# Linear attention feeding a two-layer MLP on one core: batch 1's kv put between its transposes, its denominators and scaling earlier, two loads exchanged

## The chip, the core and the metric

One core of a Trainium2 chip. Its engines run side by side, each with its own queue of instructions that it works off in order: TensorE (PE, matmuls; PEld are its weight loads), VectorE (DVE), ScalarE (ACT), GpSimd (POOL) and SyncE (SP). They meet through semaphores. Matmul results land in PSUM, which this kernel uses as 8 banks of 128 partitions by 512 float32. Transfers between DRAM and the on-chip memory go through 16 DMA engines; a transfer is put in a queue by one of the engines above, and a transfer that converts float32 to bfloat16, as all loads here do, is put in by GpSimd.

The metric is device time of the core in microseconds (us), as the median of several runs.

## The reference: what is computed

Eight batches, 8 heads, 576 positions, head size 64. First linear attention, then, with the heads laid side by side to 4608 tokens of 512 features, two matrix products with a tanh between.

```python
def phi(x):
    return np.where(x > 0, x, np.exp(x) - 1.0) + 1.0
q_p, k_p = (phi(q), phi(k))
kv = np.einsum('bhsd,bhse->bhde', k_p, v)
z = np.sum(k_p, axis=2)
num = np.einsum('bhsd,bhde->bhse', q_p, kv)
den = np.einsum('bhsd,bhd->bhs', q_p, z)[..., None] + 1e-06
x = (num / den)                      # to [4608, 512]
h = x @ w_in                         # [512, 2048]
out = (h - np.tanh(h)) @ w_out       # [2048, 512]
```

## The kernel before

**Two grids that don't match.** Attention works by batch, 576 tokens each (B = 8). The MLP works by chunk `c` of 512 tokens (NC = 9). `xT` holds the attention's result, features on partitions, in four slices `p` of 128 features: two heads each, the "pairs" of this text. Chunk 0 needs batch 0, chunk 1 needs the last 64 tokens of batch 0 and most of batch 1, and so on. So while chunk `c` runs, the attention of batch `c + 1` is made between its matmuls, and phi of batch `c + 2` is begun.

**A chunk.** Layer 1 (`l1mm`, line 366) has 16 blocks `fi`; a block is four matmuls, one for each pair `p`, into one PSUM bank. From chunk 1 on two blocks fill two neighbouring banks, ScalarE makes the tanh of both at once (line 372) and VectorE subtracts (line 373), which writes `gT` and sets the two banks free. Six banks (0 to 5) go round this way; banks 6 and 7 are attention's. Layer 2 (`l2mm`, line 387) has 16 steps `s` of four matmuls each, in lists `s2[s]` that name what is to be issued after the step. In chunk 0 the step is `(g, i)` = (`s // 4`, `s % 4`): the first four steps use the first quarter of `w_out`, steps 4 to 7 the second, steps 8 to 11 the third, steps 12 to 15 the last, and from step 12 on each step ends with a copy of a finished bank to `osb` on ScalarE (line 396) and two stores from SyncE's queue. In later chunks a bank is finished before the next is begun.

**Batch 1**, whose order is written out by hand into chunk 0's lists: phi of k and q; `a_qT_pe(1, i)` (line 157), 9 transposes on TensorE for each half `i` of q, copied out by ScalarE (line 168) and VectorE (line 170); `a_kv(1)` (line 180), 36 matmuls over k and v, masked into `kz` by VectorE (line 186); `b0_scale_rest` (line 261), the last 64 tokens of batch 0; `a_den` (line 267), 16 matmuls, an addition and a reciprocal; `num1` (line 516), 8 matmuls copied to `ns` by ScalarE; `a_split` (line 288), four VectorE instructions that split the reciprocal into parts in bfloat16; `spread1(h)` (line 511), 8 matmuls that spread the reciprocals of two pairs over the partitions (line 354), and two VectorE products (line 359) that write these pairs of `xT`. These use banks 4 to 7 in turn (`side`).

**Batch 2**, also by hand: `phi_pieces` (line 121) gives three parts for half a tensor: an exp on ScalarE (line 134), a maximum on VectorE (line 135) and a minimum on VectorE (line 136). `exp2` issues the first, `rest2` the other two. `a_qT_dma(2)` (line 151) puts a transposing DMA into SyncE's queue. A tiny GpSimd copy (`gate`, line 380) waits for it, and behind it GpSimd issues the loads of batch 3. `a_kv_cols(2)` (line 191) and `a_den(2)` follow within layer 1 of chunk 1; `a_spread` (line 301) sends the reciprocals of batch 2 through DRAM and back, and line 328 multiplies them into `xT` during layer 2 of chunk 1.

**The loads.** GpSimd's queue holds, among others and in this order: q, k, v of batch 0, `w_in`, k of batch 1, quarters 0 and 1 of `w_out`, q of batch 1, quarter 2 of `w_out`, v of batch 1, quarter 3 of `w_out`; then q, k, v of batch 2, once phi of batch 1's q is done with its buffer.

**The beginning of chunk 1.** Blocks 0 and 1 are interleaved (line 581): pairs 0 and 1 of both, then pairs 2 and 3 of both, so that the later pairs are asked for later.

Of the kernel before, what the change touches and what calls it, by code (L numbers as in the profile page):

```python
# [18 lines left out]
def kernel(  # L19
# [14 lines left out]
    NP = H // 2  # L34
# [17 lines left out]
    ps_all = psum.tile([128, 8, 512], F32, name="ps_all")  # L52
# [9 lines left out]
    dense = Banks([0, 1, 2, 3, 4, 5])  # L62
# [41 lines left out]
    def load_v(b):  # L104
        load(b, v_b[b % 2][:, 0:2], v, b == 0)
# [8 lines left out]
    def load_wo(g):  # L114
        nc.gpsimd.dma_start(out=w_out_sb[:, 4 * g:4 * g + 4, :],
                            in_=moe_w_out[512 * g:512 * g + 512, :].rearrange("(ko ki) f -> ki ko f", ki=128))
# [40 lines left out]
    def a_qT_pe(b, i, banks, on=None):  # L157
        if i == 0:
            new_qT(b)
        for n in range(2):  # L160
            j0, j1 = ((0, 5), (5, 9))[n]
            ps = banks().bitcast(BF16).rearrange("p (j t) -> p j t", t=128)
            for j in range(j0, j1):
                nc.tensor.transpose(ps[:, j - j0, :], qp_t[b][:, i, j].rearrange("p h d -> p (h d)"), ident)
            src = ps[:, 0:j1 - j0, :]
            dst = qT_t[b][:, i, j0:j1].rearrange("p j g t -> p j (g t)")
            if (on or "AV")[n] == "A":
                nc.scalar.copy(dst, src)
            else:
                nc.vector.tensor_copy(dst, src)  # L170
# [9 lines left out]
    def a_kv(b, banks):  # L180
        kz_t[b] = kz_c[b % 2]
        ps = [banks()[:, 0:384].rearrange("p (i e) -> p i e", i=2) for hg in range(2)]
        for i in range(2):
            kv_mm(b, i, [ps[hg][:, i, :] for hg in range(2)])
        for hg in range(2):
            nc.vector.tensor_mul(kz_t[b][:, hg], ps[hg][:, :, 0:160], mask[:, hg])
# [74 lines left out]
    def b0_scale_rest(banks):  # L261
        ps = num_mm(0, NP, banks)
        nc.vector.tensor_mul(
            xT[:, :, 512:576].rearrange("p a (t c) -> p a t c", t=4),
            ps[:, 0:NP, :].rearrange("p a (t c) -> p a t c", t=4), rdb_t[0])
# [22 lines left out]
    def a_split(b):  # L288

        f = rden_t[b]  # L290
        t1 = rpool.tile([128, J * 16], BF16, name="t1")
        u = rpool.tile([128, J * 16], F32, name="u")
        t2 = rpool.tile([128, J * 16], BF16, name="t2")
        w = rpool.tile([128, J * 16], BF16, name="w")
        nc.vector.tensor_copy(t1, f)
        nc.vector.scalar_tensor_tensor(u, t1, part[:, 0:1], f, ALU.mult, ALU.add)
        nc.vector.tensor_copy(t2, u)
        nc.vector.scalar_tensor_tensor(w, t2, part[:, 1:2], u, ALU.mult, ALU.add)
        rden_t[b] = w
# [118 lines left out]
    for i in (1, 0):  # L418
        nc.gpsimd.memset(v_b[i][:, 2], 1.0)
    nc.gpsimd.memset(vp[:, :, :, 128:136], 1.0)  # L420
    load_wo(2)
    load_v(1)
    load_wo(3)

    nc.vector.memset(mask, 0.0)
# [76 lines left out]
    for c in range(NC):  # L502
        gT = gpool.tile([128, NF, 512], BF16, name="gT")
        n1, n2 = c + 1, c + 2
        s1 = {i: [] for i in range(16)}
        s2 = {i: [] for i in range(16)}
        if c == 0:
            side = Banks([4, 5, 6, 7])
            sub = {}

            def spread1(h):
                sub["bp"] = a_spread_pe(1, 4, (2 * h, 2 * h + 1))
                for p in (2 * h, 2 * h + 1):
                    a_scale(1, p, sub["ns"], sub["bp"], 144 * (p % 2))

            def num1():
                sub["ns"] = new_ns(1)
                for p in (NP, 0, 1, 2, 3):
                    a_num_copy(1, sub["ns"], p, side)

            s1[11].append(lambda: a_kphi(1, 0))
            s1[13].append(lambda: a_kphi(1, 1))
            s2[3].append(lambda: a_qphi(1, 0))
            s2[4].append(lambda: (a_qphi(1, 1), load_q(2), load_k(2), load_v(2)))
            s2[0].append(prepare)
            s2[7].append(lambda: a_qT_pe(1, 0, side))
            s2[8].append(lambda: a_qT_pe(1, 1, side))
            s2[10].append(lambda: (a_kv(1, side), b0_scale_rest(side)))
            s2[11].append(lambda: (a_den(1, side), num1(), a_split(1)))
            s2[13].append(lambda: spread1(0))  # L530

            qs, ks = [], []

            def exp2(pieces, src, store, name, i):
                pieces.append(phi_pieces(2, src, store, name, i))
                pieces[i][0]()

            def rest2(f):
                f[1]()
                f[2]()  # L540

            s2[12].append(lambda: exp2(qs, q_t, qp_t, "qp", 0))
            s2[13].append(lambda: exp2(qs, q_t, qp_t, "qp", 1))
            s2[14].append(lambda: exp2(ks, k_t, kp_t, "kp", 0))
            s2[15].append(lambda: (spread1(1), rest2(qs[0]), rest2(qs[1]), a_qT_dma(2), rest2(ks[0])))
        elif n1 < B:
            s1[8 if c == 1 else 5].append(lambda: a_kv_cols(n1, attn))
            s1[10 if c == 1 else 8].append(lambda: (a_den(n1, attn), a_spread(n1)))
            for p in range(NP + 1):
                s2[(11 if c == 1 else 9) + p].append(lambda p=p: a_num(n1, p))  # L550
        if c == 1:
            s1[1].append(lambda: a_kphi(2, 1))
            s1[3].append(lambda: (a_vp(2, 0), a_vp(2, 1)))
        if c >= 1 and n2 < B:

            s1[0].append(lambda: (gate(qT_t[n1]), load_k(n2), load_q(n2), load_v(n2)))
            d = 2
            s2[d].append(lambda: a_kphi(n2, 0))
            s2[d + 2].append(lambda: a_kphi(n2, 1))
            s2[d + 4].append(lambda: a_qphi(n2, 0))  # L560
            s2[d + 6].append(lambda: (a_qphi(n2, 1), a_qT_dma(n2)))
            for i in range(2):
                s2[14 + i].append(lambda i=i: a_vp(n2, i))
        if c == 0:

            first = Banks([4, 5, 6, 7, 0, 1, 2, 3])
            hs = [ps_all[:, n, :] for n in range(4)]
            order = [((0, 0), (0, 1)), ((2, 0), (2, 1), (0, 2), (0, 3), (2, 2), (2, 3)),
                     [(p, fi) for p in (1, 3) for fi in range(4)]]
            seen = [0] * 4  # L570
            for n, part_ in enumerate(order):
                if n == 1:
                    open2()
                for p, fi in part_:
                    l1mm(c, fi, hs[fi], p, seen[fi])
                    seen[fi] += 1
            for fi in range(4):
                l1act(fi, hs[fi], gT)
        for fi in range(4 if c == 0 else 0, NF):
            h = first() if c == 0 else dense()  # L580
            if c == 1 and fi == 1:
                for two in (0, 2):
                    for f, o in ((0, ps_all[:, dense.order[(dense.n - 2) % 6], :]), (1, h)):
                        for p in (two, two + 1):
                            l1mm(c, f, o, p, p)
            elif c != 1 or fi > 1:
                for p in range(NP):
                    l1mm(c, fi, h, p, p)
            if c == 0:
                l1act(fi, h, gT)  # L590
            elif fi % 2:
                n = dense.order[(dense.n - 1) % 6]
                l1act2(fi - 1, ps_all[:, n - 1:n + 1, :], gT)
            for f in s1[fi]:
                f()
        os_ = {}
        for s in range(16):

            (g, i) = divmod(s, 4) if c == 0 else (s % 4, s // 4)
            if g == 0:  # L600
                os_[i] = ps_all[:, i, :] if c == 0 else dense()
            if c == NC - 1 and i == 3:

                if g == 0:
                    o2 = dense()
                    for o, f in ((os_[i], slice(0, 384)), (o2, slice(384, DM))):
                        for fi in range(NF):
                            nc.tensor.matmul(o[:, f], gT[:, fi, 384:512], w_out_sb[:, fi, f],
                                             start=(fi == 0), stop=(fi == NF - 1))
                        evac(c, i, o, f.start, f.stop)  # L610
                continue
            l2mm(gT, os_[i], i, 4 * g, 4 * g + 4)
            if g == 3:
                evac(c, i, os_[i])
            for f in s2[s]:
                f()
# [30 lines left out]
```

## Time and profile before

| | |
|---|---|
| median of 3 runs | 295.46 us (295.45 to 295.57) |
| the profiled execution | 295.57 us |
| its span, first to last instruction | 293.8 us |
| TensorE busy | 283.4 us |
| VectorE busy | 174.6 us |
| ScalarE busy | 139.4 us |
| GpSimd busy | 33.4 us |
| bytes moved by DMA | 38.94 MB, 133 GB/s over the span |

The span in 40 slices of 7.3 us, in tenths of busy time, for TensorE, VectorE, ScalarE and the DMA engines; the last row but one is the clock granted to TensorE:

```
PE   7899999899999999999999999999999999999994
DVE  4759948997467764786478646866581446106600
ACT  3838538747334653455246524661452155126411
PEclk9999999999999999999999999999999999999999
DMA  6999999878989658945796669767107310131032
```

A line of the timeline gives the start in us, the time from the first start to the last end, the engine, the line of the kernel, the operation, what it writes and reads, and how many instructions are merged. In brackets stand the engine's idle time before it and what ended it. "DMA_DIRECT2D" lines of POOL or SP are the issue of a transfer; the transfer lands later, and the list of DMA issues gives the time from issue to landing.

Chunk 0's layer 2 runs from 31.3 us to 50.2 us, layer 1 of chunk 1 from there to 67.6 us, and its layer 2 to 82.8 us. From then on a chunk with attention in it takes 30.4 us (113.1 to 143.5 us).

### The profile page before, as it was taken

How to read it: one execution, taken by the hardware profiler on the slowest of the kernel's cores; microseconds unless marked ns; L12 is line 12 of the kernel's file. 1: busy time of each engine (PE TensorE's matmuls, PEld its weight loads, DVE VectorE, ACT ScalarE, POOL GpSimd, SP SyncE). 2: the span in 40 equal slices, each digit the busy share in tenths (PEclk: the TensorE clock that was granted, in tenths of full speed). 3: DMA queues.
4: the chain of work that ended last, by engine and by line, in shares of the span. 5: the costliest groups of instructions: out<-in, count | busy, mean ns of one | idle time of the engine just before them, and what ended most of it. 6: DMA issues, size and time to landing. Idle time of an engine off the chain costs nothing.

```text
span 293.8 us, 4475 instructions
## 1 busy us (share of the span) xinstructions
PE 283.4 (96%) x1773; PEld 133.9 (46%) x1801; DVE 174.6 (59%) x265; ACT 139.4 (47%) x168; POOL 33.4 (11%) x55
## 2 busy tenths in 40 slices
PE   7899999899999999999999999999999999999994
PEld 2544464344445444444454445444544444444443
DVE  4759948997467764786478646866581446106600
ACT  3838538747334653455246524661452155126411
POOL 8573030030030003000300021000000000000000
PEclk9999999999999999999999999999999999999999
DMA  6999999878989658945796669767107310131032
GB/s 96 195 204 213 207 207 219 203 118 161 231 167 194 145 122 140 221 112 130 137 218 118 155 137 174 143 149 149 38 21 180 73 36 0 38 82 25 0 74 71
DMA packets 39077, 38.94 MB, mean 133 GB/s; under 512 B 16336, under 2 KB 33808, under 8 KB 38288
## 3 DMA queue, kind: packets, MB, share of 16 engines
q0 software_dynamic: 17552, 18.35, 38.6%
q1 hardware_dynamic: 21344, 20.17, 30.1%
q8 instruction: 14, 0.23, 0.3%
q10 hardware_dynamic: 160, 0.13, 0.1%
q14 instruction: 7, 0.06, 0.1%
HBM read 43.91 MB, written 9.55 MB: 182 GB/s over the span
## 4 chain that ended last, share of the span: by engine, by line
PE 80%; DMA 9%; DVE 5%; ACT 2%; issue 1%; POOL 1%; SPq 1%; DVEq 0%; ACTq 0%; POOLq 0%
PE ps_all L366 37%; PE ps_all L387 35%; DMA rdb<-ds 3%; DMA v<-in_v_dram 2%; DMA out_dram<-osb 2%; PE ps_all L199 2%; PE ps_all L317 2%; DMA ds<-rden 1%; PE ps_all L276 1%; DVE gT L378 1%; DVE gT L373 1%; ACT th L377 1%; ACT osb L396 1%; PE ps_all L177 1%; DVE qp L136 1%
## 5 line engine op out<-in xcount | busy, mean ns | idle before, releaser
L366 PE MATMUL ps_all<-xT,w_in_sb 128*128 128x512 bf16 x561 | 127.5, 379 | 2.5 <-DVE gT L373 1.1
L387 PE MATMUL ps_all<-w_out_sb,gT 128*128 128x512 bf16 x547 | 126.0, 379 | 0.7
L373 DVE TENSOR_TENSOR gT<-ps_all,th 128x1024 bf16<-128x1024 f32 x64 | 77.9, 1218 | 59.3 <-ACT th L372 59.3
L372 ACT ACTIVATE th<-ps_all 128x1024 f32<-128x1024 f32 x64 | 65.5, 1024 | 58.4 <-PE ps_all L366 45.4
L366 PEld LDWEIGHTS <-w_in_sb 128*128 128x128 bf16 x576 | 55.1, 98 | 68.4 <-issue 3.0
L387 PEld LDWEIGHTS <-gT 128*128 128x128 bf16 x560 | 54.2, 98 | 64.5 <-issue 0.5
L396 ACT COPY osb<-ps_all 128x512 f32<-128x512 f32 (+1 forms) x36 | 21.2, 589 | 72.4 <-PE ps_all L387 56.0
L328 DVE TENSOR_TENSOR xT<-ps_all,rdb 128x512 bf16<-128x512 f32 x24 | 16.3, 690 | 13.8 <-PE ps_all L317 11.2
L134 ACT ACTIVATE e<-qraw 128x1152 bf16<-128x1152 bf16 x16 | 18.6, 1168 | 6.7 <-DMA qraw<-in_q_dram 6.7
L134 ACT ACTIVATE e<-kraw 128x1152 bf16<-128x1152 bf16 x15 | 17.5, 1166 | 0.4 <-DMA kraw<-in_k_dram 0.4
L136 DVE TENSOR_TENSOR qp<-e,r 128x1152 bf16<-128x1152 bf16 x16 | 12.1, 758 | 8.1 <-ACT e L134 7.3
L136 DVE TENSOR_TENSOR kp<-e,r 128x1152 bf16<-128x1152 bf16 x15 | 11.4, 758 | 7.9 <-ACT e L134 7.0
L383 POOL COPY g<-qT 1x1 bf16<-1x1 bf16 x5 | 1.2, 241 | 121.4 <-DMA qT<-qp 121.4
L378 DVE TENSOR_TENSOR gT<-ps_all,th 128x512 bf16<-128x512 f32 x16 | 10.3, 686 | 2.4 <-ACT th L377 1.7
L377 ACT ACTIVATE th<-ps_all 128x512 f32<-128x512 f32 x16 | 9.2, 599 | 4.3 <-PE ps_all L366 3.1
L317 PE MATMUL ps_all<-qT,kz 128*128 128x512 bf16 x28 | 10.1, 379 | 0.2 <-DVE xT L328 0.2
L444 PE MATMUL ps_all<-zero 128*128 128x512 bf16 x29 | 8.3, 443 | 1.2 <-DVE zero L405 1.2
L135 DVE TENSOR_SCALAR r<-qraw 128x1152 bf16<-128x1152 bf16 x16 | 7.3, 454 | 2.1 <-DMA qraw<-in_q_dram 2.1
L199 PEld LDWEIGHTS <-kp 64*128 64x128 bf16 x216 | 6.4, 94 | 2.5 <-issue 2.1
L285 DVE RECIPROCAL rden<-den 128x144 f32<-128x144 f32 x7 | 7.4, 1053 | 0.2
L199 PE MATMUL ps_all<-vp,kp 64*128 64x136 bf16 x216 | 7.4, 220 | 0.0
L394 DVE COPY osb<-ps_all 128x128 f32<-128x128 f32 x1 | 0.3, 292 | 11.6 <-DMA out_dram<-osb 11.6
(82 smaller groups left out, 121.5 us busy)
## 6 DMA issues: line engine op xcount, KB each, us to landing
out_dram<-osb SPq DMA_DIRECT2D x70, 128.0 KB
rdb<-ds SPq DMA_DIRECT2D x12, 576.0 KB
kraw<-in_k_dram POOLq DMA_DIRECT2D x7, 576.0 KB, 7.1
qraw<-in_q_dram POOLq DMA_DIRECT2D x7, 576.0 KB, 9.1
v<-in_v_dram POOLq DMA_DIRECT2D x7, 576.0 KB, 12.2
w_out_sb<-in_moe_w_out_dram POOLq DMA_DIRECT2D x4, 512.0 KB, 15.0
w_in_sb<-in_moe_w_in_dram POOLq DMA_DIRECT2D x6, 256.0 KB, 8.6
qraw<-in_q_dram POOLq DMA_DIRECT2D x2, 288.0 KB, 4.7
```

What stands on the lines that cost most here:

```text
L134: return (lambda: nc.scalar.activation(e, x, AF.Exp), lambda: nc.vector.tensor_scalar(r, x, 0.0, 1.0, ALU.max, ALU.add), lambda: nc.vector ...
L136: lambda: nc.vector.tensor_tensor(y, e, r, ALU.min))
L199: nc.tensor.matmul(ps[hg][:, i, :], kp[r, i, j].rearrange("p h d -> p (h d)"), vp[r, i, j, :], start=(j == 0), stop=(j == J - 1))
L317: nc.tensor.matmul(ps, kz[:, p // 2, p % 2, 0:128], qT[:, p % 2, 0:8, p // 2, :], start=True, stop=True)
L328: nc.vector.tensor_mul(xT[:, p, S * b:S * b + 512].rearrange("p (j t c) -> p j t c", j=8, t=4), ps.rearrange("p j (t c) -> p j t c", t=4), ...
L366: nc.tensor.matmul(h, w_in_sb[:, 2 * (p % 2) + p // 2, fi * 128:(fi + 1) * 128], xT[:, p, c * 512:(c + 1) * 512], start=(n == 0), stop=(n ...
L372: nc.scalar.activation(th, h, AF.Tanh)
L373: nc.vector.tensor_sub(gT[:, fi:fi + 2, :], h, th)
L377: nc.scalar.activation(th, h, AF.Tanh)
L378: nc.vector.tensor_sub(gT[:, fi, :], h, th)
L387: nc.tensor.matmul(o, gT[:, fi, i * 128:(i + 1) * 128], w_out_sb[:, fi, :], start=(fi == 0), stop=(fi == NF - 1))
L396: nc.scalar.copy(osb[:, f0:f1], o[:, f0:f1])
```

## The change

The two loads change places. In chunk 0's lists, kv of batch 1 goes between the two groups of transposes and all three go behind step 7 (before: transposes behind steps 7 and 8, kv behind step 10). The rest of batch 0 goes from behind step 10 to behind step 8, den, num and split from 11 to 9, the spreads from 13 and 15 to 11 and 13. Of batch 2, exp of q's first half goes from behind step 12 to behind 11, q's second from 13 to 12, k's first from 14 to 13; the VectorE parts, which all came behind step 15 after the second spread's products, now come behind the step of their exp or the one after, q's first half ahead of the second spread's products; the transposing DMA goes from behind step 15 to behind step 13, ahead of the stores of two finished banks. In chunk 1, blocks 0 and 1 of layer 1 are no longer interleaved. No instruction is added or taken away on any engine.

```diff
+    load_v(1)
     load_wo(2)
-    load_v(1)
     load_wo(3)
...
-            s2[7].append(lambda: a_qT_pe(1, 0, side))
-            s2[8].append(lambda: a_qT_pe(1, 1, side))
-            s2[10].append(lambda: (a_kv(1, side), b0_scale_rest(side)))
-            s2[11].append(lambda: (a_den(1, side), num1(), a_split(1)))
-            s2[13].append(lambda: spread1(0))
+            s2[7].append(lambda: (a_qT_pe(1, 0, side), a_kv(1, side), a_qT_pe(1, 1, side)))
+            s2[8].append(lambda: b0_scale_rest(side))
+            s2[9].append(lambda: (a_den(1, side), num1(), a_split(1)))
+            s2[11].append(lambda: spread1(0))
...
-            s2[12].append(lambda: exp2(qs, q_t, qp_t, "qp", 0))
-            s2[13].append(lambda: exp2(qs, q_t, qp_t, "qp", 1))
-            s2[14].append(lambda: exp2(ks, k_t, kp_t, "kp", 0))
-            s2[15].append(lambda: (spread1(1), rest2(qs[0]), rest2(qs[1]), a_qT_dma(2), rest2(ks[0])))
+            s2[11].append(lambda: (exp2(qs, q_t, qp_t, "qp", 0), rest2(qs[0])))
+            s2[12].append(lambda: exp2(qs, q_t, qp_t, "qp", 1))
+            s2[13].append(lambda: (spread1(1), exp2(ks, k_t, kp_t, "kp", 0), rest2(qs[1]), a_qT_dma(2)))
+            s2[14].append(lambda: rest2(ks[0]))
...
-            if c == 1 and fi == 1:
-                for two in (0, 2):
-                    for f, o in ((0, ps_all[:, dense.order[(dense.n - 2) % 6], :]), (1, h)):
-                        for p in (two, two + 1):
-                            l1mm(c, f, o, p, p)
-            elif c != 1 or fi > 1:
-                for p in range(NP):
-                    l1mm(c, fi, h, p, p)
+            for p in range(NP):
+                l1mm(c, fi, h, p, p)
```

## The prediction

> **What bounds the kernel now.** I read the busy line and the chain first, then the timelines of TensorE (PE) and VectorE (DVE) where the diff acts, 38 to 63 us, then the landings of the loads, then TensorE from 63 us to the end for what could swallow a gain.
>
> ```profile
> PE 283.4 (96%) x1773; PEld 133.9 (46%) x1801; DVE 174.6 (59%) x265; ACT 139.4 (47%) x168; POOL 33.4 (11%) x55
> PE 80%; DMA 9%; DVE 5%; ACT 2%; issue 1%; POOL 1%; SPq 1%; DVEq 0%; ACTq 0%; POOLq 0%
> ```
>
> TensorE is the bound: only its pauses can be won or lost. From 98.31 to 106.94 us 40 dense matmuls start in a row, so one takes 8.63 / 40 = 0.2158 us from start to start (the 0.38 us printed for one overlaps its neighbours). With that pitch I find the pauses; the bracketed idle time is 0.16 us short of each.
>
> ```profile
> 38.19 0.67 PE L164 MATMUL ps_all<-ident,qp 128*128 128x128 bf16 x9
> 41.88 1.66 PE L177 MATMUL ps_all<-v,kp 64*128 64x192 bf16 x36
> 44.56 0.43 PE L276 MATMUL ps_all<-qT,kz 128*32 128x144 bf16 x16
> 47.85 0.30 PE L354 MATMUL ps_all<-w,sel 32*128 32x144 bf16 x8
> 50.15 1.30 PE L366 MATMUL ps_all<-xT,w_in_sb 128*128 128x512 bf16 x5
> 51.74 4.26 PE L366 MATMUL ps_all<-xT,w_in_sb 128*128 128x512 bf16 x19 [0.29 <-DVE xT L359]
> 56.58 1.89 PE L366 MATMUL ps_all<-xT,w_in_sb 128*128 128x512 bf16 x8 [0.57 <-DVE gT L373]
> 58.94 1.02 PE L366 MATMUL ps_all<-xT,w_in_sb 128*128 128x512 bf16 x4 [0.48 <-DVE gT L373]
> 62.90 0.43 PE L276 MATMUL ps_all<-qT,kz 128*32 128x144 bf16 x16
> 80.48 0.38 PE L317 MATMUL ps_all<-qT,kz 128*128 128x512 bf16 x1 [0.20 <-DVE xT L328]
> ```
>
> Chunk 1 begins at 50.15. Five matmuls end their turn at 50.15 + 5 x 0.2158 = 51.23, the next starts at 51.74: 0.51 lost, waiting for scaled xT of pair 3. Then 51.74 + 19 x 0.2158 = 55.84 against 56.58: 0.74 lost; 56.58 + 8 x 0.2158 = 58.31 against 58.94: 0.63 lost; both wait until VectorE's L373 frees a pair of banks. Another 0.10 goes before L199 at 59.90. Sum 1.98 us. VectorE shows why:
>
> ```profile
> 48.27 1.42 DVE L359 TENSOR_TENSOR xT<-ns,ps_all 128x576 bf16<-128x576 f32 x2 [0.48 <-PE ps_all L354]
> 50.27 1.42 DVE L359 TENSOR_TENSOR xT<-ns,ps_all 128x576 bf16<-128x576 f32 x2 [0.58 <-PE ps_all L354]
> 55.31 1.22 DVE L373 TENSOR_TENSOR gT<-ps_all,th 128x1024 bf16<-128x1024 f32 x1
> 57.67 1.22 DVE L373 TENSOR_TENSOR gT<-ps_all,th 128x1024 bf16<-128x1024 f32 x1
> ```
>
> From 50.27 it has no gap until past 60 us: two scales, three phi pieces, L373, a phi piece, L373. It idles 0.58 us before 50.27, and its whole load hangs on when the spreads (L354) come. After 63 us TensorE has one pause worth naming, at 80.48: the step before starts at 79.25, four matmuls end at 80.11, so 0.37 is lost until the reciprocals have come back from DRAM (L328).
>
> **The loads.** They come down GpSimd's queue in order:
>
> ```profile
> 22.59 0.75 POOL L115 DMA_DIRECT2D w_out_sb<-in_moe_w_out_dram  x1
> 23.32 0.76 POOL L93 DMA_DIRECT2D v<-in_v_dram  x1
> ...
> w_out_sb<-in_moe_w_out_dram POOLq DMA_DIRECT2D x1, 512.0 KB, 15.8
> v<-in_v_dram POOLq DMA_DIRECT2D x1, 576.0 KB, 17.9
> ```
>
> Issue plus landing: q of batch 1 at 19.70 + 16.1 = 35.80, third quarter of w_out at 22.59 + 15.8 = 38.39, v of batch 1 at 23.32 + 17.9 = 41.22, last quarter at 24.05 + 19.7 = 43.75. So w_out takes 2.59 after its forerunner and v takes 2.83.
>
> **The change, part by part.** Swapping the two loads puts v at 35.80 + 2.83 = 38.63 and the third quarter at 41.22; the last quarter stays at 43.75, and q, k, v of batch 2 behind it keep their 46.6, 49.6 and 52.6. TensorE's work is the same set of matmuls in another order, so I walk it. First transposes at 38.19 as before, done 38.70. kv (36 matmuls, 41.88 to 43.48 = 1.60, and 0.09 lead-in): v has landed 0.07 earlier; done 40.39. Its waits for the copies out of the transposes' banks (ScalarE, VectorE done by 39.4) lie under it. Second transposes to 40.89. Step 8 needs the third quarter: 41.22 and a wake-up of 0.04, (q of batch 1: landed 35.80, used 35.83), so 41.26, **a new pause of 0.37**. Behind it in TensorE's queue stand step 8 and everything else. Step 8 to 42.12, four small matmuls for the rest of batch 0 (0.12), step 9 to 43.10, den from 43.15 (44.56 before). VectorE's masks of kz and the second copy of qT are done by 41.7, so nothing waits for them. Rest of num 0.12 and four num 0.86, steps 10 and 11: 46.2. The spread comes 47.85 - 44.56 = 3.29 after den (reciprocal and split), at 46.44; the pause of 0.2 there is as large before (45.92 + 8 x 0.2158 = 47.65 against 47.85), so it cancels. Steps 12, 13 to 48.40, second spread 0.23, steps 14, 15 to 50.36: chunk 1 starts **0.21 later** than 50.15, the 0.37 less the small waits that go.
>
> VectorE starts its scales 0.42 after the spread (48.27 - 47.85), at 46.86, and is past two at 48.16. Then the new order puts phi of q ahead of the other two: 1.23 a piece (51.61 to 52.84). Its exp needs q at 46.6 and 1.16 on ScalarE, done 47.8, so nothing is late; if q came after 47.6 the delay would pass to pair 2. Scales of pairs 2 and 3 from 49.4 to 50.8. TensorE wants them at 50.36 + 0.43 = 50.79 and 51.01, and they are there at 50.1 and 50.8: so the interleaving of the first two blocks goes at no cost, on a slack of 0.2; without it the price is again some tenths. Then phi to 53.15, L373 from 53.3 (its tanh ends 53.3, after the output copies of ScalarE), phi, L373 from 55.66 to 56.88. TensorE needs these banks at 50.36 + 24 x 0.2158 = 55.54 (free at 54.5) and 57.27 (free at 56.88). No pause. The copies of v end 57.6, ahead of L199 at 58.1. den of batch 2 starts at 61.13 instead of 62.90: **1.77 earlier** = 1.98 - 0.21. ScalarE's exps move ahead of output copies; its queue then runs 46.6 to 55.2 nearly full, with 0.3 to spare before the tanh. SyncE's transpose of q passes four store issues and starts at 52.0 instead of 54.23; the stores behind its 2.81 us feed only free output buffers. The gate at L383 and the loads of batch 3 follow some 2 us earlier, beside a chain of den that is 1.8 earlier too.
>
> What the trace does not show is the round trip of the reciprocals in its new place. Before: reciprocal done 65.73, landed in DRAM 71.06, back at 79.6. It starts 1.8 earlier and so do the loads it shares the engines with. Bounds: landing unmoved takes all 1.77 back; the pause of 0.37 gone gives 2.14. I take the same pause, since both shift together. The third quarter's landing is bounded by 38.4 and 43.75, the landings about it; I take 41.22, the sum of spacings.
>
> A rule that speaks against the change. The granted clock stood at 1.00 through transposes and small matmuls:
>
> ```profile
> 39.00:42.00 3.00, 3.00 (x25) 1.51 (x25) 0.78 (x3) 1.06 (x2) 1.92 (x3) 1.00 1.23 207
> 42.00:45.00 3.00, 2.95 (x62) 2.06 (x60) 1.22 (x3) 0.00 (x0) 0.00 (x0) 1.00 1.22 207
> ```
>
> (length, PE, PEld, DVE, ACT, POOL busy, clock, DMA share, GB/s.) The Trainium skill, "TensorE: Matmul & The Clock Gate", section "What's actually happening", has the clock halve after an idle window of about 3.4 us, and its Part 4 says that transposes do not count as busy. From 38.19 to 41.26 the new order has 3.07 us without a dense matmul, so the page leaves it just warm; should it trip, an estimate by that page is some 1.7 us lost, and the sum would be near zero. The trace has no such stretch, and I keep 1.00.
>
> **Sum.** The profiled execution took 295.57: span 293.80 and 1.77 around it. Minus 1.77 is 293.80; the median of the runs, 295.46, is 0.11 below the profiled one, so the forecast is 293.7.
>
> **Rivals.** (1) The round trip decides. At 80.48 TensorE already waits for it, which speaks for; that the chain and its competing loads both start about 2 us earlier speaks against. Half the shift lost gives 294.6, all of it 295.46: no change. (2) Slower: v keeps its landing. TensorE's queue is in order, and kv now stands ahead of steps 8 to 11, which before ran under that load. Each tenth that v comes after 39.0 (38.63 and the slack of 0.37) costs a tenth; past 40.8 the change loses. At the old 41.22 kv ends at 42.96, transposes 43.46, step 8 is 2.20 late: 293.7 + 2.2 = 295.9. Seven landings in queue order, 2.3 to 2.9 apart, speak against it; that TensorE arrives 0.07 after the estimate speaks for it.
>
> **How the numbers follow.** A measurement of this kernel tells about 0.2% (0.6 us) from no change. Forecast 0.62, its own range 293.2 (a smaller round-trip pause) to 294.4 (some tenths at the thin margins). Rival 1 gets 0.18: 0.10 still faster, 0.08 no change. Rival 2 gets 0.20, slower or a hair under. Faster 0.72, same 0.08, slower 0.20. The range runs to 295.8, over rival 1 and the near part of rival 2, and down to 293.1.
>
> **What would show it.** Right: L177 from about 38.7, one pause near 41.2 on the third quarter, no bracket on L373 before L366 between 50 and 60 us, L276 of batch 2 near 61.1, every later stage 1.8 earlier. Wrong: L177 well past 39; scales of pair 3 after 51.0; a longer wait for L328 near 78; a clock under 1.00 about 41 us.

## The result, and the profile after

| | before | after |
|---|---|---|
| median | 295.50 us (295.45 to 295.57, 4 runs) | 293.98 us (293.58 to 294.60, 4 runs) |
| the profiled execution | 295.57 us, span 293.8 us | 293.58 us, span 291.8 us |

The ratio is 0.995, with a 95% interval of 0.9929 to 0.9971: 1.5 us faster. Over all three sets of the changed kernel (15 executions, the experiments' among them) the median is 294.01.

The page's line of busy time, and its chain by engine:

```profile
PE 283.9 (97%) x1772; PEld 134.2 (46%) x1801; DVE 174.7 (60%) x265; ACT 139.6 (48%) x168; POOL 33.4 (11%) x55
PE 81%; DMA 14%; POOL 2%; issue 1%; ACT 1%; SPq 0%; DVE 0%; POOLq 0%
```

The work is the same; the span around it is 2.0 us shorter. VectorE, 5% of the chain before, has gone from it. In its place stands DMA with 14%: the chain now goes back from step 8 to the landing of the third quarter of `w_out`. The timeline of TensorE of the changed kernel, at the places shown of before:

```profile
37.78 0.67 PE L164 MATMUL ps_all<-ident,qp 128*128 128x128 bf16 x9
38.58 1.66 PE L177 MATMUL ps_all<-v,kp 64*128 64x192 bf16 x36
40.17 0.68 PE L164 MATMUL ps_all<-ident,qp 128*128 128x128 bf16 x9
41.08 1.02 PE L387 MATMUL ps_all<-w_out_sb,gT 128*128 128x512 bf16 x3 [0.24 <-DMA w_out_sb<-in_moe_w_out_dram]
...
46.30 0.30 PE L354 MATMUL ps_all<-w,sel 32*128 32x144 bf16 x8
...
50.34 7.93 PE L366 MATMUL ps_all<-xT,w_in_sb 128*128 128x512 bf16 x35
58.21 1.24 PE L199 MATMUL ps_all<-vp,kp 64*128 64x136 bf16 x36
...
61.21 0.43 PE L276 MATMUL ps_all<-qT,kz 128*32 128x144 bf16 x16
...
78.48 0.38 PE L317 MATMUL ps_all<-qT,kz 128*128 128x512 bf16 x1
```

What to see: the four stretches of L366 between 50 and 60 us, with a bracket between each, have become one line of 7.93 us that no bracket cuts (36 matmuls at 0.2158 take 7.77 from start to start, and one record is missing). The new pause stands at 41.08, with its DMA named: the transposes end their turn at 40.17 + 0.51 = 40.68, so 0.40 are lost. VectorE's timeline shows why the others went:

```profile
46.73 1.42 DVE L359 TENSOR_TENSOR xT<-ns,ps_all 128x576 bf16<-128x576 f32 x2 [0.48 <-PE ps_all L354]
48.06 0.45 DVE L135 TENSOR_SCALAR r<-qraw 128x1152 bf16<-128x1152 bf16 x1
...
49.30 1.41 DVE L359 TENSOR_TENSOR xT<-ns,ps_all 128x576 bf16<-128x576 f32 x2
...
53.33 1.23 DVE L373 TENSOR_TENSOR gT<-ps_all,th 128x1024 bf16<-128x1024 f32 x1
...
55.70 1.22 DVE L373 TENSOR_TENSOR gT<-ps_all,th 128x1024 bf16<-128x1024 f32 x1
```

The scales start 1.54 earlier than at 48.27, the gap of 0.58 between their pairs is filled with a phi piece, and L373 starts 1.98 earlier, while chunk 1 starts 0.19 later. The loads, from the list of DMA issues (v issued at 22.46, the quarter at 23.19):

```profile
v<-in_v_dram POOLq DMA_DIRECT2D x1, 576.0 KB, 16.1
w_out_sb<-in_moe_w_out_dram POOLq DMA_DIRECT2D x1, 512.0 KB, 17.9
```

They land at 38.56 and 41.09 by these rounded figures, and TensorE's kv and step 8 start at 38.58 and 41.08: between 38 and 41 us TensorE follows the load queue. One thing shows how firmly. In this execution k and v of batch 0 landed some 0.4 earlier than in the profile of before, so chunk 0's layer 2 began at 30.88 instead of 31.29 and the first transposes came at 37.78 instead of 38.19. Nothing of it was left at 41.08: kv, due at 37.78 + 0.51 + 0.09 = 38.38, waited 0.20 for v, and step 8 the 0.40.

### The profile page after: what moved, and what is told of

Its sections match the earlier page's. It is cut to its first block, busy times and chain, and to the rows that moved or that the text cites. A ratio compares the mean times of both kernels' runs of the same rounds, so it can differ in the third digit from the quotient of the medians.

```text
span 291.8 us, 4470 instructions
## 1 busy us (share of the span) xinstructions
PE 283.9 (97%) x1772; PEld 134.2 (46%) x1801; DVE 174.7 (60%) x265; ACT 139.6 (48%) x168; POOL 33.4 (11%) x55
## 4 chain that ended last, share of the span: by engine, by line
PE 81%; DMA 14%; POOL 2%; issue 1%; ACT 1%; SPq 0%; DVE 0%; POOLq 0%
PE ps_all L366 38%; PE ps_all L387 37%; DMA w_out_sb<-in_moe_w_out_dram 6%; DMA w_in_sb<-in_moe_w_in_dram 3%; DMA out_dram<-osb 2%; PE ps_all L199 2%; DMA kraw<-in_k_dram 2%; PE ps_all L317 2%; PE ps_all L276 1%; POOL v L419 1%; ACT osb L396 1%; SPq L401 0%; POOL qraw L90 0%; PE ps_all L320 0%; POOL qraw L93 0%
## 5 line engine op out<-in xcount | busy, mean ns | idle before, releaser
L366 PE MATMUL ps_all<-xT,w_in_sb 128*128 128x512 bf16 x560 | 127.1, 380 | 1.1 <-DVE xT L244 0.3
L373 DVE TENSOR_TENSOR gT<-ps_all,th 128x1024 bf16<-128x1024 f32 x64 | 77.9, 1218 | 59.8 <-ACT th L372 59.6
L366 PEld LDWEIGHTS <-w_in_sb 128*128 128x128 bf16 x576 | 55.1, 98 | 66.8 <-issue 0.6
L328 DVE TENSOR_TENSOR xT<-ps_all,rdb 128x512 bf16<-128x512 f32 x24 | 16.3, 690 | 13.5 <-PE ps_all L317 13.5
L444 PE MATMUL ps_all<-zero 128*128 128x512 bf16 x29 | 9.2, 482 | 1.2 <-DVE zero L405 1.2
L317 PE MATMUL ps_all<-qT,kz 128*128 128x512 bf16 x28 | 10.1, 380 | 0.0
L199 PEld LDWEIGHTS <-kp 64*128 64x128 bf16 x216 | 6.4, 94 | 2.5 <-issue 2.5
L199 PE MATMUL ps_all<-vp,kp 64*128 64x136 bf16 x216 | 7.4, 220 | 0.0
```

The lines of the kernel that those rows point to most:

```text
L199: nc.tensor.matmul(ps[hg][:, i, :], kp[r, i, j].rearrange("p h d -> p (h d)"), vp[r, i, j, :], start=(j == 0), stop=(j == J - 1))
L317: nc.tensor.matmul(ps, kz[:, p // 2, p % 2, 0:128], qT[:, p % 2, 0:8, p // 2, :], start=True, stop=True)
L328: nc.vector.tensor_mul(xT[:, p, S * b:S * b + 512].rearrange("p (j t c) -> p j t c", j=8, t=4), ps.rearrange("p j (t c) -> p j t c", t=4), ...
L366: nc.tensor.matmul(h, w_in_sb[:, 2 * (p % 2) + p // 2, fi * 128:(fi + 1) * 128], xT[:, p, c * 512:(c + 1) * 512], start=(n == 0), stop=(n ...
L373: nc.vector.tensor_sub(gT[:, fi:fi + 2, :], h, th)
```

## The experiments

Every kernel was timed beside the kernel before on the same chip; a ratio is to that one. "The changed kernel" is the version of the diff.

### 1. The changed kernel again, twice

No edit.

> The changed kernel once more, to see how far its times spread (293.58 to 294.60 in four runs, where the kernel before kept within 0.12). Theory: TensorE now meets v of batch 1 and the third quarter of w_out as they land, so the spread of the landings passes to the end: 293.6 to 294.6 again, and if the profiled execution falls high, step 8 starts later than 41.08 us by as much. Rival: the first four runs were a matter of that chip or hour: all within 0.2 of each other.

> The changed kernel, as the measure for the two variants run beside it: 293.9, with a pause of some 0.35 to 0.4 before step 8 and of 0.1 to 0.3 before kv.

Measured: 293.85 (293.44 to 294.35), ratio 0.9945 [0.9932, 0.9957], and 294.01 (293.56 to 294.34), ratio 0.9953 [0.9942, 0.9965]. The gain is firm. The theory of the spread isn't borne out: beside these the kernel before spread from 294.95 to 295.89 and from 295.07 to 295.75, as wide as the changed one, though nothing in it waits for v or the third quarter. Its 0.12 in the first runs were the exception. In the profiles of the two kv starts at 38.74 and 38.81 and step 8 at 41.19 and 41.14, den of batch 2 at 61.31 and 61.27. There the transposes came later (38.15 and 38.21), so kv did not wait for v, against the second expectation, and the pause before step 8 was 0.35 and 0.23.

### 2. The loads in their old order, the rest as changed (run twice)

```diff
-    load_v(1)
     load_wo(2)
+    load_v(1)
     load_wo(3)
```

> The changed kernel with the third quarter of w_out ahead of v of batch 1 again, the rest as changed. Theory (loads land in queue order, and kv now stands first in TensorE's queue): kv starts at 41.2 instead of 38.58, step 8 at 43.4 instead of 41.08, everything later: 294.0 + 2.3 = 296.3. Rival (the two loads are served side by side, the order matters little): within 0.5 of the changed kernel.

> The changed kernel with the loads in their old order once more. In six runs it took 295.8 to 296.2 twice and 297.4 to 297.7 four times, and the granted clock fell to 0.991 to 0.994 in the latter. Theory: the pause of 2.5 before kv, with transposes on one side and kv on the other, lets the clock fall to half for one stretch of some 3.5 us in which TensorE loses 1.6 to 1.8; if the profiled execution is of these, the rows show the clock at 0.5 between 41 and 49 us and matmuls of twice the time. Rival: the clock falls only behind the last matmul, and the 1.6 come from later landings: then kv starts near 42.6.

Measured: 297.37 (295.79 to 297.66), ratio 1.0059 [1.0042, 1.0077], and 297.34 (295.92 to 297.58), ratio 1.0061 [1.0044, 1.0078]. The timeline of TensorE in the first:

```profile
41.07 1.66 PE L177 MATMUL ps_all<-v,kp 64*128 64x192 bf16 x36 [2.51 <-DMA v<-in_v_dram]
...
43.17 1.03 PE L387 MATMUL ps_all<-w_out_sb,gT 128*128 128x512 bf16 x4
...
52.44 7.93 PE L366 MATMUL ps_all<-xT,w_in_sb 128*128 128x512 bf16 x36
```

kv waits for v by name, and step 8 is 2.1 late: landing follows queue order, as the theory had it (it forecast 296.3; the medians are 1 us above that). That accounts for the profiled execution, 295.79, which is 2.1 above the 293.65 of the changed kernel's profile beside it. But both profiled executions were the fastest of their six, and eight of the twelve took about 1.5 more, each with a mean granted clock of 0.991 to 0.994 where the four others have 0.997 to 1.00. The second run was to catch one of these in its profile and didn't, so where the clock fell in them is not shown; experiment 3 was made for it.

### 3. v of batch 1 behind both quarters: a longer pause

```diff
-    load_v(1)
     load_wo(2)
     load_wo(3)
+    load_v(1)
```

> The changed kernel with v of batch 1 behind both last quarters of w_out, so that kv waits longer still: v lands near 43.6, kv starts there after a pause of 5.2, step 8 near 45.8, 4.7 later than in the changed kernel. Theory (a pause of this length always lets the clock fall): the granted clock shows 0.5 in the rows from some point after 41 us, matmuls of twice the time follow for up to 4 us, and the whole is 294.0 + 4.7 + 1.7 = 300.4. Rival (the clock has no part in it): 298.7, clock 1.00 throughout.

Measured: 300.39 (300.04 to 301.37), ratio 1.0174 [1.0159, 1.0190]. The table by stretches has length, busy time of PE, PEld, DVE, ACT and POOL, the granted clock, the share of DMA and GB/s:

```profile
38.00:40.00 2.00, 0.77 (x10) 0.50 (x9) 1.50 (x4) 0.99 (x2) 1.06 (x2) 1.00 1.24 207
40.00:42.00 2.00, 0.00 (x0) 0.00 (x0) 0.00 (x0) 0.00 (x0) 1.17 (x2) 1.00 1.21 208
42.00:44.00 2.00, 0.00 (x0) 0.00 (x0) 0.00 (x0) 0.00 (x0) 0.00 (x0) 0.71 1.22 208
44.00:46.00 2.00, 1.97 (x26) 1.86 (x28) 0.00 (x0) 0.00 (x0) 0.00 (x0) 0.50 1.21 207
46.00:48.00 2.00, 2.00 (x24) 1.66 (x21) 0.88 (x2) 0.22 (x1) 0.00 (x0) 0.50 1.21 206
48.00:50.00 2.00, 1.78 (x10) 0.79 (x10) 0.45 (x3) 0.47 (x1) 0.00 (x0) 0.58 1.21 209
50.00:52.00 2.00, 2.00 (x28) 0.97 (x27) 1.15 (x3) 0.56 (x2) 0.00 (x0) 1.00 0.57 100
```

and from its timeline of TensorE:

```profile
44.03 3.06 PE L177 MATMUL ps_all<-v,kp 64*128 64x192 bf16 x36 [5.26 <-DMA v<-in_v_dram]
47.03 1.14 PE L164 MATMUL ps_all<-ident,qp 128*128 128x128 bf16 x9
```

The clock falls to half within the pause. A mean of 0.71 means that 0.58 of the stretch from 42 to 44 was at 0.5, so it fell at 42.84, and 0.58 from 48 to 50 means that it came back at 49.68: 6.8 us at half speed, in which the 36 matmuls of kv take 3.06 instead of 1.66. den of batch 1 starts at 50.74 against 43.02, 7.7 later: 5.45 are the later start of kv, less the 0.40 of the pause before step 8 that no longer occurs, and 2.7 are the clock. The forecast of 300.4 was met by the median alone: the profiled execution, 301.37, is the slowest, and in it both terms were larger (5.05 instead of 4.7 for the later start, 2.7 instead of 1.7 for the clock). All four executions have a mean clock of 0.986 or 0.987. So a pause of 5.3 brought the clock down in all four; the pause of 2.5 in experiment 2, by the mean clocks of its list, in eight executions of twelve.

### 4. The kernel before, with the loads exchanged

```diff
-    load_wo(2)
     load_v(1)
+    load_wo(2)
     load_wo(3)
```

> The kernel before with only the two loads exchanged. Theory: step 8, which stands between its two groups of transposes, waits for the third quarter until 41.1 instead of starting at 38.7, v is early for nothing, all else 2.3 later: 297.7, and up to 1.6 more in executions where the clock falls. So neither the loads nor the order of the matmuls gains alone. Rival (an earlier v is what gains): below 295.4.

Measured: 298.58 (297.60 to 299.88), ratio 1.0111 [1.0090, 1.0131]; the profiled execution 297.60, the lowest; three of six have a mean clock of 0.993, and with 298.95 to 299.88 they are the three slowest.

```profile
40.97 1.02 PE L387 MATMUL ps_all<-w_out_sb,gT 128*128 128x512 bf16 x4 [2.75 <-DMA w_out_sb<-in_moe_w_out_dram]
...
54.01 4.26 PE L366 MATMUL ps_all<-xT,w_in_sb 128*128 128x512 bf16 x19 [0.29 <-DVE xT L359]
58.84 1.89 PE L366 MATMUL ps_all<-xT,w_in_sb 128*128 128x512 bf16 x8 [0.57 <-DVE gT L373]
```

Step 8 waits, and the brackets of the kernel before come back to the hundredth, 2.27 later. In experiment 2, with the new order, they are absent (one line of 7.93 from 52.44) although all there is 2 us late as well: they belong to the order of the work, not to when the loads land. By the medians the new order alone loses 1.9 and 2.0 us (experiment 2), the new loads alone 3.3, and both together gain 1.5. Without the fall of the clock the new order alone loses little: its four other executions, 295.79 to 296.16, lie 0.3 to 0.7 above the medians of the kernel before.

### 5. VectorE's part of phi behind the scales again

```diff
-            s2[11].append(lambda: (exp2(qs, q_t, qp_t, "qp", 0), rest2(qs[0])))
+            s2[11].append(lambda: exp2(qs, q_t, qp_t, "qp", 0))
...
-            s2[13].append(lambda: (spread1(1), exp2(ks, k_t, kp_t, "kp", 0), rest2(qs[1]), a_qT_dma(2)))
+            s2[13].append(lambda: (spread1(1), exp2(ks, k_t, kp_t, "kp", 0), rest2(qs[0]), rest2(qs[1]), a_qT_dma(2)))
```

> The changed kernel with VectorE's part of phi of q's first half behind the scales of pairs 2 and 3, all else as changed. Theory: VectorE then idles some 0.7 between the two pairs of scales, everything behind is 0.46 later, L373 of blocks 2 and 3 ends 57.4 instead of 56.92 and block 8 waits some 0.2: plus 0.2, 294.2. Rival (phi ahead of the scales is what brought the gain): plus 0.7 or more, with L373 waits like those before. Second rival (it does not matter at all): no bracket on L373 before L366, same time.

Measured: 294.16 (293.93 to 294.41), ratio 0.9955 [0.9943, 0.9967]; 0.15 to 0.3 above the changed kernel, within what the intervals leave open. The profile shows two effects of it:

```profile
50.68 8.08 PE L366 MATMUL ps_all<-xT,w_in_sb 128*128 128x512 bf16 x36
...
79.31 0.38 PE L317 MATMUL ps_all<-qT,kz 128*128 128x512 bf16 x1 [0.24 <-DVE xT L328]
```

The run of layer 1 is 8.08 instead of 7.93, so 0.15 are lost within it, for L373 of blocks 2 and 3 ends 57.69 and block 8 is due at 50.68 + 32 x 0.2158 = 57.59. That is little more than what varies: two profiles of experiment 8, with phi in its new place, show 8.03 and 8.00. And the pause at L317 is back: the transposing DMA is issued at 53.03 instead of 52.02, and the loads of batch 3 go with it. Of this 1.01 the edit, by the later second half of q's phi, brings 0.67; for 0.34 this whole profile is later, since step 8 got its quarter at 41.42 instead of 41.08.

### 6. The transposing DMA behind the stores again

```diff
-            s2[13].append(lambda: (spread1(1), exp2(ks, k_t, kp_t, "kp", 0), rest2(qs[1]), a_qT_dma(2)))
+            s2[13].append(lambda: (spread1(1), exp2(ks, k_t, kp_t, "kp", 0), rest2(qs[1])))
             s2[14].append(lambda: rest2(ks[0]))
+            s2[15].append(lambda: a_qT_dma(2))
```

> The changed kernel with the transposing DMA of batch 2 behind step 15 and all eight stores, as before; the gate and the loads of batch 3 then start some 2 us later (near 59.5), the denominators of batch 2 don't. Theory: the pause before L317 fell from 0.37 to 0.06 since the competing loads moved by 2.2 and the reciprocals by 1.7, so with late loads the round trip ends later: a pause of 0.3 to 1.3, 294.3 to 295.3. Rival (the round trip does not mind these loads): L328 starts near 77.7 as now, same time.

Measured: 294.22 (293.92 to 295.35), ratio 0.9962 [0.9947, 0.9977].

```profile
79.20 0.38 PE L317 MATMUL ps_all<-qT,kz 128*128 128x512 bf16 x1 [0.47 <-DVE xT L328]
```

The step before starts at 77.71, its four matmuls end at 78.57, so 0.63 are lost here; in the changed kernel 77.56 + 0.86 = 78.42 against 78.48, 0.06. Four profiles side by side:

| kernel | loads of batch 3 start | reciprocal ends | L328 starts | from reciprocal to L328 |
|---|---|---|---|---|
| changed | 57.33 | 64.03 | 77.74 | 13.71 |
| before | 59.50 | 65.73 | 79.73 | 14.00 |
| experiment 5 | 58.33 | 64.52 | 78.57 | 14.05 |
| experiment 6 | 59.81 | 64.19 | 78.46 | 14.27 |

In these four, the longer the lead of the loads over the reciprocal (6.7, 6.2, 6.2 and 4.4 us), the shorter the round trip. The other profiles don't bear the trend out: in nine of them, with a lead of 6.5 to 6.8, the trip took 13.44 (the second of experiment 1) to 14.02 (the second with both loads in halves, experiment 8), and in experiment 4, with a lead of 6.2, 13.82. Only the 14.27 lies clearly outside that spread. So loads that start 2.5 us later lengthened the trip in this one profile; the differences among the other three rows are no larger than what varies by itself, and the medians move by 0.2 to 0.4 only.

### 7. Blocks 0 and 1 interleaved again

The lines that the diff takes out are put back.

> The changed kernel with blocks 0 and 1 of chunk 1 interleaved again. Theory: pairs 2 and 3 of xT are there at 50.05 and 50.72, TensorE asks for them at 50.77 and 50.98 without the interleaving, so it buys nothing: 293.9, the same within 0.2. Rival (the slack of 0.2 is gone in many executions): 0.2 to 0.4 faster than the changed kernel.

Measured: 293.83 (293.34 to 294.22), ratio 0.9949 [0.9937, 0.9962], and layer 1 again one line without a bracket:

```profile
50.05 7.93 PE L366 MATMUL ps_all<-xT,w_in_sb 128*128 128x512 bf16 x35
```

The time is the same within 0.2, as the theory had it: the interleaving has nothing left to hide.

### 8. The two loads in halves

```diff
+    def load_wo_half(g, n):
+        f = 4 * g + 2 * n
+        nc.gpsimd.dma_start(out=w_out_sb[:, f:f + 2, :],
+                            in_=moe_w_out[128 * f:128 * f + 256, :].rearrange("(ko ki) f -> ki ko f", ki=128))
...
     load_v(1)
-    load_wo(2)
+    load_wo_half(2, 0)
+    load_wo_half(2, 1)
```

> The changed kernel with the third quarter of w_out loaded as two halves, two slices of 128 rows each. Theory (step 8 waits for the last bytes of the quarter alone): its first two matmuls need only the first half, which lands 1.25 earlier (half of the 2.5 that a quarter takes), so the pause before step 8 goes: minus 0.35. Rival (an added transfer costs the queue its set-up time, or halves land together): no gain.

and with v of batch 1 in halves too:

```diff
-        load(b, v_b[b % 2][:, 0:2], v, b == 0)
+        load(b, v_b[b % 2][:, 0:2], v, b <= 1)
```

> The same, and v of batch 1 in two halves as well, of which kv uses the first in its first 18 matmuls. Theory: the pause before kv goes too where there is one (0.1 to 0.3), but step 8 then meets the second half of the quarter as it lands: minus 0.35 to 0.5 against the changed kernel. Rival: kv's weights wait for both halves, no gain over the variant with one split.

> The variant with both loads in halves once more: its five runs lay at 293.27 to 293.91 and those of the changed kernel beside it at 293.56 to 294.34, which overlap. Theory: den of batch 2 starts near 60.95 (61.2 to 61.3 in the changed kernel), 293.4 to 293.6, a ratio to the kernel before of 0.9935 to 0.9945. Rival: 293.9, and the first five were luck.

Measured: 293.74 (293.51 to 294.15), ratio 0.9947 [0.9935, 0.9959] with one split; 293.42 (293.27 to 293.91), ratio 0.9939 [0.9927, 0.9951] and 293.67 (293.33 to 294.07), ratio 0.9936 [0.9923, 0.9950] with both. With one split step 8 follows the transposes at 40.81 without a pause, as the theory had it; the gain of 0.27 beside the changed kernel is not clear of the spread. From the first profile with both (the added lines move the numbers by 5: L392 is `l2mm`):

```profile
40.08 0.68 PE L169 MATMUL ps_all<-ident,qp 128*128 128x128 bf16 x9
40.59 1.22 PE L392 MATMUL ps_all<-w_out_sb,gT 128*128 128x512 bf16 x4
...
60.98 0.43 PE L281 MATMUL ps_all<-qT,kz 128*32 128x144 bf16 x16
```

Step 8 follows the transposes without a pause, but its four matmuls take 1.22 instead of 1.03: the second half of the quarter lands in the midst of them. den of batch 2 comes 0.2 to 0.3 earlier. In the second profile the first transposes came late, at 38.44; neither kv nor step 8 waited, and den came at 61.27, so that profile misses the 60.95 expected. The medians of all executions, 293.64 in ten against 294.01 in fifteen, speak for 0.4, with ranges that overlap, so that the gain is likely and not shown. By its medians it is the fastest version tried, 1.9 us below the kernel before in both runs.

## Why the prediction was right

**The bound and the three pauses.** Right: all three of chunk 1 are gone. The 0.10 before L199, which the sum of 1.98 counted with them, is not: 50.34 + 36 x 0.2158 = 58.11 against 58.21. It was no pause but a lead-in, as the prediction itself gives kv 0.09. From the start of chunk 1 to den of batch 2 the changed kernel takes 61.21 - 50.34 = 10.87; before it was 12.75, so 1.88 were won, the 1.98 less this 0.10. Experiments 2 and 4 show that the order of the work does it.

**The new pause and the later chunk 1.** Right in place and releaser: 0.40 against 0.37, with 0.35 and 0.23 in the two profiles of experiment 1. The spacing of landings in the queue held: v 38.56 for 38.63, the quarter 41.09 for 41.22. That chunk 1 starts at 50.34 (50.36 foreseen) is in part luck: step 8 began 0.18 earlier than forecast, and from there to chunk 1 it took 9.26 instead of 9.10, since the walk left out lead-ins such as the 0.10 before the second spread (46.54 + 8 x 0.2158 = 48.27 against 48.37).

**VectorE's new order.** Right: scales at 46.73 (46.86), L373 at 53.33 (53.3) and 55.70 (55.66), its banks free 0.3 ahead of need. The phi piece between the scales is worth little by itself: at most 0.15 within layer 1, by experiment 5; the end of the interleaving is worth nothing, by experiment 7. That the earlier spreads bring the rest is argued, from the timeline and because the other parts fall away; no run puts the spreads alone back to their old steps.

**den of batch 2.** 61.21 instead of 61.13: 1.69 earlier against 1.77, by the 0.10 before L199 less 0.02.

**The round trip.** The step taken, that its pause of 0.37 stays, was wrong by 0.31: in the profile 0.06 are left, and 0.04 and 0.01 in those of experiment 1, which is nearly the better bound. The loads of batch 3 moved by 2.17 and the reciprocal by 1.70. Experiment 6 gives the pause back by putting the transposing DMA, and with it the loads, later; but 0.38 came back in the second profile of both loads in halves with the loads as early, and 0.17 is all that experiment 4 shows with the old order. So what took the 0.31 stays open. The profiled time fell by 1.99, which is 1.69 and 0.31 but for the rounding.

**The sum.** 293.7 forecast, 293.98 measured. The profiled execution, 293.58, was the fastest of its four, and the medians of the changed kernel lie 0.2 to 0.45 above their profiled executions in all three sets. What these other executions lose is not shown, since only one of each set has a trace. One reason why the medians differ by less than the two profiles (1.5 against 2.0) can be estimated, but is not shown: in the kernel before, v had landed at 41.22 and kv came at 41.88, so first loads that land 0.4 earlier would pass on to its end, and the changed kernel loses them at 41.08. Beside an execution of before with such loads its gain would be near 1.6.

**The rivals.** The round trip did not decide. Slower through v: v did land early, and the price of this rival was right in its mechanism and too low in its size. Experiment 2 put v back to its old landing; step 8 came at 43.17 (43.46 by the rival's walk), the profiled time was 295.79 (295.9 foreseen), yet the median was 297.37, with a lower mean clock in most executions, which the price left out.

**The clock.** The Trainium skill, "TensorE: Matmul & The Clock Gate", section "What's actually happening", spoke against the change with its idle window of about 3.4 us. The changed kernel has 41.08 - 37.78 = 3.3 us without a dense matmul, and no execution of 15 shows a mean clock under 0.998. Experiment 3 shows the clock at half within a pause of 5.3, and by the mean clocks it fell in four of four. In experiment 2, 5.3 us without a dense matmul (37.89 to 43.17), half of it a pause, go with a lower mean clock in eight of twelve. The runs agree with the rule as far as they reach; where its limit lies between 3.3 and 5.3 us, and which small matmuls count as idle, they don't show, so the change stays on the right side by a margin that was not measured.

## What to carry to other kernels

Where TensorE is the bound, look for the engine that frees its banks and ask what starts that engine's busy stretch: moving three pieces of work two steps earlier, and (for at most 0.15 us of it) filling one gap of 0.6 us, removed three pauses that named VectorE, at the price of one that names a load. An order of work and an order of loads belong together: each half of this change alone lost 1.9 us or more by the medians. And a pause must be priced with the clock: with one of 2.5 us beside transposes and small matmuls, two executions of three had a lower mean clock and took another 1.5 us.

## What the runs showed of the hardware that was not expected

After the clock had fallen it took TensorE long to get it back: in experiment 3 kv starts at 44.03 and the clock returns at 49.68, after 5.65 us in which TensorE had hardly a pause (its one bracket, 0.22, stands where the record of one of step 8's four matmuls is missing), and in which only the last 1.7 us held dense matmuls. The same section of the skill names some 3.4 us of sustained work for the way back; whether the half-empty matmuls and transposes of those 5.65 us don't count, or the window fell badly, one trace can't tell.

And executions of one kernel on one core differ by up to 1 us without any sign in the mean clock, before and after alike (294.95 to 295.89, 293.44 to 294.35). Profiles of the same kernel differ by 0.4 in when the first loads have landed.
